# Attention with beacons, then soft experts: other first loads and beacon loads, a reordered start, row sums among the output

## The chip, the cores and the metric

One NeuronCore of a Trainium2 chip runs one program. It has five engines with instruction streams of their own: TensorE (PE, with its weight loads as PEld), VectorE (DVE), ScalarE (ACT), GpSimd (POOL) and SyncE (SP), and 16 DMA engines that move data between HBM and SBUF on behalf of queues: SP's, ACT's and POOL's. PE reads SBUF and writes PSUM; DVE and ACT read and write both; POOL works on SBUF. The metric is the device time of one execution in microseconds; lower is better. TensorE's clock is granted in steps and shown by the profile (1.00 is full).

## The reference

Eight batches of eight heads, 576 tokens, 64 channels, with 16 beacon keys and values ahead of the causal ones:

```python
k_all = concatenate([beacon_k, k], axis=2)          # (8, 8, 592, 64)
v_all = concatenate([beacon_v, v], axis=2)
scores = q @ k_all.T / 8                            # causal mask on the 576, none on the beacons
a = exp(scores - max); a /= a.sum + 1e-9
x = (a @ v_all)  -> (4608, 512)                     # heads side by side

logits = x @ phi                                    # (4608, 32): 8 experts of 4 slots
d = softmax of logits over the 4608 tokens;  c = softmax over the 32 slots
slot_out[e] = relu((d.T @ x)[e] @ w1[e]) @ w2[e]    # w1 (512, 1024), w2 (1024, 512), per expert
out = c @ slot_out                                  # (4608, 512)
```

All inputs and the output are float32: q, k and v 9.4 MB each, the experts' weights 33.6 MB, the output 9.4 MB.

## The kernel before

The kernel keeps q, k and the scores' exponentials in half precision and takes no maximum; a flag computed at the end chooses a general path if the sums ever leave their range. The work on x is laid out by pairs of heads: 32 pairs (`n`), four to a batch (`b, g = divmod(n, 4)`). The order of all five instruction streams is written out by hand (`tc.manual_schedule`, L666): what is emitted first on an engine runs first there, and SP and POOL issue their DMAs in the same way, in order.

**Loads.** `load_qk(b, hb)` (L344) brings k and q of four heads, two heads a row of partitions, as 2304 byte pieces on 128 partitions. `load_v(b)` (L355) brings v so that partition p holds four successive rows of every head, shifted by the 16 beacon rows; partitions 0 to 3 are the beacons' place. For batch 0 it asks for partitions 4 to 116 and 116 to 128, for the others for all 128, whose first four are then overwritten by `load_bv(b)` (L380), 32 KB on 4 partitions. As that overwrites, SP waits for v before it issues it. `load_vr` (L376) brings the last 80 rows in 256 byte pieces. The beacon keys of all batches come once, on 64 partitions (L669). The expert weights are cast from float32 on the way, 32 requests of 512 KB (in float16) on POOL's queue (`load_weights`, L442), one or two after each pair; the last 12 go into buffers that q, k and v no longer need (`wt`, `wv`).

**Start (L699 to L744).** PE first runs `fill` matmuls without use of their result, turns k and q of the first half batch (`transposes`, L466: PE into PSUM tiles of the tag "tr", of which there are two, then DVE and ACT back to SBUF), turns the beacon keys through PSUM into `bkA` (L712), from which POOL copies the 16 columns of each pair ahead of k (`beacon_keys`, L459). Then come scores and exponentials of pairs 0 and 1, four banks each (`scores`, L508: PE, then ACT's exp from a "sc" tile, of which there are two; `select`, L497: POOL masks). v is cast by POOL (`cast_v`, L384, pieces 0, 1 and the remainder 2) and its rows are put in token order by `perm_v` (L396): 16 matmuls with quarter-array 0/1 matrices `sel` into four banks, then ACT and DVE copy to `vh`.

**Loop (L746).** For n = 2 to 31: scores of pair n, transposes of a later half batch, the weighted sums of pair n-1 (`attend`, L525), their division (`normalize`, DVE), turning x (`x_transposes`), once a batch the logits (L572), the slots' inputs (`dispatch`, L604) and the turned weights `eT` (`combine_T`, L636); casts and `perm_v` of the next batch at g = 1 to 3 (for batch 1 at g = 2 and 3, that is at pairs 2 and 3); loads of batch b+2 at g = 0 and 2.

**End.** After the last pair PE does the first expert products (`first`), turns them, does the second ones (`second`, L827) into `so`, which DVE divides into `so1` (L863). `row_sums(bb)` (L659) computes the softmax denominators of a quarter of the tokens, nine matmuls of one column; `row_factors` (L840) turns two quarters at a time into reciprocals. The output stage (L901) is 36 matmuls, each scaled by ACT or DVE into `osb` (six buffers) and stored by SP in 13 requests. POOL's range tests (L880) run beside it, and `judge` (L891) combines them.

## Time and profile before

| | |
|---|---|
| Time, median of 3 runs | 203.09 us (202.74 to 204.77) |
| The profiled execution | 203.09 us, of which the span 201.4 us |
| Busy: PE, DVE, ACT, POOL | 163.2, 132.2, 133.9, 113.9 us |
| Granted TensorE clock, mean | 0.95 |
| HBM read, written | 62.69 MB, 9.44 MB |
| DMA, mean over the span | 278 GB/s |
| First exponential of pair 0, of pair 2 | 12.20, 23.81 us |
| Start of the output's matmuls | 171.86 us |

Times inside the execution count from the start of the span. GB/s are bytes written by the DMA engines: a weight load that casts reads twice what it counts. A line such as "POOL L390 CAST vc<-vstag 128x512 f16<-128x512 f32 x4" names the engine, the line of the kernel, the operation, what is written from what, the shapes, and how many instructions were merged; in brackets stands the idle time before and what ended it.

### The profile page before, as it was taken

The page shows a single profiled execution, that of the slowest core. Times are in us where ns is not written, and L with a number is a line of the kernel's source. Part 1 is how long each engine was busy: PE and PEld are TensorE (multiplying, and loading weights), DVE is VectorE, ACT ScalarE, POOL GpSimd, SP SyncE. Part 2 cuts the span into 40 slices and gives each one's busy share as a digit, 9 for nine tenths or more (in the row PEclk, how much of TensorE's full clock was granted, in tenths as well). Part 3 has the DMA queues.
Part 4 walks back from the last instruction along what each step waited for, and adds up shares of the span by engine and source line. Part 5 has one row for each costly group of instructions (what it writes and reads, how often), then busy time and mean ns, then how long its engine had stood idle before and what let it go on. Part 6 is the DMA issues. An engine that isn't in the chain of part 4 may idle for free.

```text
span 201.4 us, 7361 instructions
## 1 busy us (share of the span) xinstructions
PE 163.2 (81%) x3121; PEld 107.9 (54%) x3121; DVE 132.2 (66%) x275; ACT 133.9 (66%) x172; POOL 113.9 (57%) x263
## 2 busy tenths in 40 slices
PE   6798893889889898988988899898989997966200
PEld 2433661668567476666756667675767753522000
DVE  0352784688987888887887878878837332898300
ACT  2355784689878888889887788987895230774200
POOL 6049186469649757865965786898786000890000
PEclk9999999799999999999999999999999999995855
DMA  6999999999999999999999999999999991499991
GB/s 206 254 244 365 278 361 317 270 370 311 267 271 378 264 261 349 292 275 305 356 232 279 379 273 268 264 219 217 211 216 212 213 202 30 176 410 417 408 405 78
DMA packets 29701, 55.90 MB, mean 278 GB/s; under 512 B 7228, under 2 KB 15644, under 8 KB 29660
## 3 DMA queue, kind: packets, MB, share of 16 engines
q1 hardware_dynamic: 24764, 37.98, 55.4%
q0 software_dynamic: 4608, 16.78, 41.7%
q10 hardware_dynamic: 288, 0.59, 1.0%
q8 instruction: 26, 0.43, 0.8%
q14 instruction: 15, 0.12, 0.2%
HBM read 62.69 MB, written 9.44 MB: 358 GB/s over the span
## 4 chain that ended last, share of the span: by engine, by line
PE 60%; DMA 10%; ACT 9%; DVE 8%; POOL 3%; issue 3%; SPq 0%; ACTq 0%; DVEq 0%; POOLq 0%
PE sc L514 15%; PE av L535 15%; PE trps L483 9%; DMA wt<-in_moe_w_dram 7%; ACT expT L519 5%; PE xtps L561 5%; DVE osb L918 4%; ACT vh L407 4%; PE vpt L404 2%; DMA kstag<-in_k_dram 2%; PE fill L655 2%; PE fps L911 2%; PE lgps L580 2%; PE vps L404 2%; PE sips L619 2%
## 5 line engine op out<-in xcount | busy, mean ns | idle before, releaser
L519 ACT ACTIVATE expT<-sc 128x992 f16<-128x992 f32 (+3 forms) x128 | 104.8, 867 | 20.6 <-PE sc L514 20.0
L505 POOL TENSOR_SCALAR_AFFINE_SELECT expT<-expT 128x224 f16<-128x224 f16 (+3 forms) x128 | 54.9, 439 | 40.1 <-ACT expT L519 39.2
L514 PE MATMUL sc<-qT,kT 64*128 64x80 bf16 (+4 forms) x576 | 43.8, 246 | 10.8 <-ACT expT L519 5.5
L535 PE MATMUL av<-vh,expT 128*128 128x65 f16 (+1 forms) x960 | 40.4, 195 | 0.4 <-DVE x L549 0.2
L535 PEld LDWEIGHTS <-expT 128*128 128x128 f16 (+1 forms) x960 | 33.7, 98 | 4.5 <-POOL expT L505 0.6
L495 DVE COPY kT<-trps 128x640 bf16<-128x640 bf16 (+1 forms) x31 | 22.7, 773 | 19.8 <-PE trps L483 19.3
L514 PEld LDWEIGHTS <-kT 64*128 64x128 bf16 x576 | 17.0, 95 | 28.1 <-issue 22.2
L495 DVE COPY qT<-trps 128x640 bf16<-128x640 bf16 (+1 forms) x30 | 22.0, 774 | 8.2 <-PE trps L483 6.3
L549 DVE TENSOR_TENSOR x<-av,r 128x640 f16<-128x640 f32 x32 | 26.4, 825 | 1.1
L390 POOL CAST vc<-vstag 128x512 f16<-128x512 f32 x32 | 18.6, 611 | 1.8 <-DMA vstag<-in_beacon_v_dram 1.8
L916 ACT ACTIVATE osb<-fps,rc 128x512 f32<-128x512 f32 (+1 forms) x18 | 11.0, 678 | 12.2 <-PE fps L911 10.9
L568 DVE COPY xT<-xtps 128x576 f16<-128x576 f16 x31 | 14.2, 457 | 6.5 <-PE xtps L561 6.5
L561 PE MATMUL xtps<-idh,x 128*128 128x128 f16 (+2 forms) x160 | 14.1, 216 | 1.1 <-issue 1.0
L918 DVE TENSOR_SCALAR osb<-fps,rc 128x512 f32<-128x512 f32 (+1 forms) x19 | 12.8, 731 | 1.3 <-PE fps L911 1.1
L655 PE MATMUL fill<-eT,onesh 128*128 128x512 f16 x35 | 11.4, 453 | 1.7 <-POOL onesh L684 1.5
L407 ACT ACTIVATE vh<-vps 128x1024 f16<-128x1024 f32 x8 | 8.2, 1027 | 6.6 <-PE vpt L404 6.6
L561 PEld LDWEIGHTS <-x 128*128 128x128 f16 (+2 forms) x160 | 9.0, 97 | 6.6 <-issue 6.0
L410 DVE CAST vh<-vpt 128x512 f16<-128x512 f32 x16 | 10.3, 685 | 3.4 <-PE vpt L404 3.4
L911 PE MATMUL fps<-so,eT 128*128 128x512 f16 (+1 forms) x37 | 11.6, 433 | 0.5 <-DVE stat L841 0.3
L462 POOL COPY kT<-bkA 64x32 bf16<-64x32 bf16 x32 | 7.4, 231 | 7.9 <-DVE bkA L712 6.9
L483 PE MATMUL trps<-idb,kstag 128*64 128x128 bf16 x270 | 11.6, 234 | 0.1
L483 PE MATMUL trps<-idb,qstag 128*64 128x128 bf16 x270 | 10.7, 222 | 0.5 <-DVE vh L410 0.4
(98 smaller groups left out, 186.7 us busy)
## 6 DMA issues: line engine op xcount, KB each, us to landing
kstag<-in_k_dram SPq DMA_DIRECT2D x15, 576.0 KB, 9.4
qstag<-in_q_dram SPq DMA_DIRECT2D x15, 576.0 KB, 13.4
out_dram<-osb SPq DMA_DIRECT2D x11, 768.0 KB, 7.6
vstag<-in_v_dram SPq DMA_DIRECT2D x7, 1024.0 KB, 15.3
w1h<-in_moe_w_dram POOLq DMA_DIRECT2D x10, 512.0 KB, 8.6
w2h<-in_moe_w_dram POOLq DMA_DIRECT2D x10, 512.0 KB, 8.5
wt<-in_moe_w_dram POOLq DMA_DIRECT2D x8, 512.0 KB, 12.2
wv<-in_moe_w_dram POOLq DMA_DIRECT2D x4, 512.0 KB, 11.6
```

Of the source, the lines that this page charges most:

```text
L390: nc.gpsimd.tensor_copy(out=st["c", b][:, :, hs, :].rearrange("p t h d -> p h t d"), in_=st["v", b][:, hs, :, :])
L407: nc.scalar.activation(vhs[b % 2][:, 0:2, :, 0:D], ps[:, :, :].rearrange("p c (h d) -> p c h d", d=D), AF.Copy)
L483: nc.tensor.transpose(tp[lo:hi, j - j0, :], t[:, hh, j, :].bitcast(BF)[:, 1::2], idb[:, :])
L495: nc.vector.tensor_copy(out=do, in_=ti)
L505: nc.gpsimd.affine_select(out=ap, in_=ap, compare_op=AL.is_ge, fill=0.0, base=cbase, pattern=pat, channel_multiplier=-1)
L514: nc.tensor.matmul(sc[:, hh, col:col + qw], kTs[n // 2 % 2][po:po + D, n % 2, c * P:(c + 1) * P], qTs[n // 2][po:po + D, n % 2, q0:q0 + qw ...
L519: nc.scalar.activation(ex[:, :, base:base + w], sc[:, :, 0:w], AF.Exp, scale=scale)
L535: nc.tensor.matmul(av[:, i, :], exps[n % 2][0:KW[c], hh, o:o + P], vhs[b % 2][0:KW[c], c, h, :], start=(c == 0), stop=(c == i))
L549: nc.vector.tensor_tensor(out=xs[b][:, :, head(n, 0):head(n, 1) + 1:head(n, 1) - head(n, 0), :].rearrange("p i h d -> p h i d"), in0=av[:, ...
L561: nc.tensor.transpose(tp[:, QLO[i]:QLO[i] + QW[i]], xs[b][0:QW[i], i, 2 * t:2 * t + 2, :].rearrange("p h d -> p (h d)"), idh[0:QW[i], 0:QW ...
L911: nc.tensor.matmul(f[:, 0:hw], row_tokens(bb, j), so1[:, hw * i:hw * i + hw], start=True, stop=True)
L918: nc.vector.tensor_scalar(out=ou, in0=f[:, 0:hw], scalar1=rc[:, bb, j:j + 1], scalar2=None, op0=AL.mult)
```

## The change

- `load_v(0)` asks for heads 1 to 7 on all 128 partitions in one request, and for head 0 in two (partitions 4 to 64, 64 to 128); POOL clears head 0's first four partitions. No beacon value is written into v's tile any more: `load_bv` is gone.
- The beacon values come twice on their own: those of batch 0 on 16 partitions (`bv0`), those of all batches on 128 (`bvf`, 256 byte pieces). POOL casts each into `bvh`, the second at pair 3. `sel` loses the rows of the first four partitions, and `perm_v` gets one more matmul, which adds the beacon rows from `bvh`.
- The beacon keys come on 128 partitions, half as long; DVE alone casts them, ahead of q's copy; 16 transposes instead of 32. The first pair's 16 columns are copied by DVE straight from PSUM, `bkA` is filled afterwards.
- SP's order: k and q of batch 1's first half ahead of its v.
- At the start: q's first transposes go into the "av" banks, as does batch 0's `perm_v`; the second piece of batch 0's v is cast by DVE; `perm_v(0)` comes right behind the first scores of pair 1; fewer fills; `sel` is built ahead of the first fill.
- The exponential of the logits is written once by ACT and copied three times by DVE in every batch, not only in the last.
- `row_sums` has its own PSUM tile and computes its reciprocals at once. Quarters 2 and 3 move from around `second(1)` into the output stage, behind the third request of quarters 0 and 1. POOL's test of the sums moves behind the other two tests, into `judge`.
- The last weight piece is asked for in two requests. One fill more ahead of the last `x_transposes`.

```diff
     def load_v(b):
...
-        if b:
...
-        else:
-            for p0, p1 in ((4, 116), (116, 128)):
+        h0 = 0 if b else 1
+        lo = ((b * H + h0) * S - Nb) * D
+        nc.sync.dma_start(
+            out=t[:, h0:H, :, :].rearrange("p h t d -> p h (t d)"),
+            in_=v.rearrange("b h s d -> (b h s d)")[lo:lo + (H - h0) * S * D].rearrange(
+                "(h e) -> h e", h=H - h0)[:, 0:4 * P * D].rearrange("h (p e) -> p h e", p=P))
+        if b == 0:
+            nc.gpsimd.memset(t[0:4, 0, :, :], 0.0)
+            for p0, p1 in ((4, 64), (64, 128)):
                 nc.sync.dma_start(
...
-    def load_bv(b):
...
-                nc.gpsimd.tensor_copy(
+                (nc.vector if c == 1 and b == 0 else nc.gpsimd).tensor_copy(
...
     def perm_v(b):
-        ps = ps_sc.tile([P, 2, 512], FP, name="vps", tag="sc")
+        pool, tag = (ps_sc, "sc") if b else (ps_av, "av")
+        ps = pool.tile([P, 2, 512], FP, name="vps", tag=tag)
...
+            if t == 0:
+                lhsT, rhs = (idh[:, b::B], bvh) if b else (idh[0:Nb, 0:Nb], bvh[0:Nb])
+                nc.tensor.matmul(outs[0][0:Nb, :], lhsT, rhs[:, :, :].rearrange("p h d -> p (h d)"),
+                                 start=False, stop=False)
...
+                cs = 2 if (e, m, j) == WLAST else 4
+                for c in range(0, 4, cs):
+                    nc.gpsimd.dma_start(
...
-        if t0 == 0:
-            nc.scalar.activation(dTs[b][:, :, :, :],
-                                 lp[:, :, :].unsqueeze(2).broadcast_to([P, NC5, 4, NSL]), AF.Exp)
-        else:
...
+        nc.scalar.activation(dTs[b][:, :, 0, :], lp[:, :, :], AF.Exp)
+        nc.vector.tensor_copy(
+            out=dTs[b][:, :, 1:4, :],
+            in_=dTs[b][:, :, 0:1, :].broadcast_to([P, NC5, 3, NSL]))
...
+    def row_sums(bb, rsp):
         for j in range(NJ):
...
+        sl = slice(bb * NJ, bb * NJ + NJ)
+        nc.vector.tensor_scalar(out=rsv[:, sl], in0=rsp[:, 0:NJ], scalar1=1e-9, scalar2=None,
+                                op0=AL.add)
+        nc.vector.reciprocal(out=rcf[:, sl], in_=rsv[:, sl])
...
         load_v(0)
-        load_bv(0)
+        bv0 = work.tile([P, H, D], FP, name="bv0", tag="x")
+        nc.sync.dma_start(out=bv0[0:Nb, :, :], in_=beacon_v[0].rearrange("h n d -> n h d"))
         load_vr(0)
         load_qk(0, 1)
+        load_qk(1, 0)
         load_v(1)
-        load_qk(1, 0)
-        load_bv(1)
         load_vr(1)
+        bvf = work.tile([P, H, D], FP, name="bvf", tag="x")
+        nc.sync.dma_start(out=bvf[:, :, :], in_=beacon_v.rearrange("b h n d -> n b h d"))
...
         fill(10, False)
         transposes(0, 0)
-        fill(2, False)
+        bkh = work.tile([P, Nb // 2, D], BF, name="bkh", tag="vc", bufs=1)
+        nc.vector.tensor_copy(out=bkh[:, :, :], in_=bkf[:, :, :].bitcast(BF)[:, :, 1::2])
         transposes(0, 1)
...
+        beacon_keys(0, bkp[:, :, :].rearrange("p n (c a) -> p n c a", a=2), nc.vector)
+        nc.vector.tensor_copy(out=bkA[:, :, :, :].rearrange("p n c a -> p n (c a)"),
+                              in_=bkp[:, :, :])
+        fill(3)
...
-        for c in range(2):
-            cast_v(0, c)
+        cast_v(0, 0)
+        nc.gpsimd.tensor_copy(out=bvh[0:Nb, :, :], in_=bv0[0:Nb, :, :])
+        cast_v(0, 1)
...
         cast_v(0, 2)
-        for bank in range(3):
-            fill(3, False)
-            scores(1, bank)
+        scores(1, 0)
+        perm_v(0)
+        scores(1, 1)
         transposes(1, 0)
-        perm_v(0)
+        scores(1, 2)
+        attend(0, 0)
+        transposes(1, 1)
         scores(1, 3)
-        transposes(1, 1)
-        attend(0, 0)
         attend(0, 1)
...
+            if n == 3:
+                nc.gpsimd.tensor_copy(out=bvh[:, :, :], in_=bvf[:, :, :])
...
-        fill(1)
+        fill(2)
...
-        row_sums(2)
         second(1)
...
-        row_sums(3)
-        row_factors(2 * NJ, 4 * NJ)
...
+        test(so1, Dm, -SUM_HI)
+        test(sz1, NDC * NSL, -SUM_HI)
         def judge():
+            test(stat, NST + 36 + 1, SUM_LO)
...
                 nc.sync.dma_start(out=outr[bb, :, j0:j1, :], in_=osb[:, 0:j1 - j0, :])
+                if bb in (0, 1) and j0 == 3:
+                    row_sums(bb + 2, ps_g.tile([P, NJ], FP, name="rsps", tag="g"))
```

More of the change, by code (lines that the diff above doesn't have):

```diff
@@ L308 @@
     phih = const.tile([P, NDC, NSL], F16, name="phih")
-    bkA = const.tile([P, Nb, B * H], BF, name="bkA")
+    bkA = const.tile([P, Nb // 2, B * H, 2], BF, name="bkA")
+    bvh = const.tile([P, H, D], F16, name="bvh")
     NRES = 5
@@ L476, in transposes @@
             dst = kTs[m % 2][:, :, Nb:Nb + S]
+        if (m, which) == (0, 1):
+            two = ps_av.tile([P, 2, 512], FP, name="trps", tag="av")
         for j0, j1 in ((0, 5), (5, NJ)):
-            tp = ps_tr.tile([P, j1 - j0, P], BF, name="trps", tag="tr")
+            if (m, which) == (0, 1):
+                tp = two[:, j0 // 5, :].bitcast(BF)[:, 0:(j1 - j0) * P].rearrange(
+                    "p (j s) -> p j s", s=P)
+            else:
+                tp = ps_tr.tile([P, j1 - j0, P], BF, name="trps", tag="tr")
             for j in range(j0, j1):
@@ L686 @@
         make_identity(nc, idh)
+        nc.gpsimd.memset(sel[:, :, :], 0.0)
         for t in kTs:
@@ L695 @@
         nc.gpsimd.memset(xT[:, :, S:640], 0.0)
-        nc.gpsimd.memset(sel[:, :, :], 0.0)
-        fill(10, False)
-        transposes(0, 0)
-        fill(2, False)
-        transposes(0, 1)
-        bkh = work.tile([P, Nb, D], BF, name="bkh", tag="vc", bufs=1)
-        hi = bkf[0:B * H, :, :].bitcast(BF)[:, :, 1::2]
-        nc.scalar.activation(bkh[0:B * H, 8:Nb, :], hi[:, 8:Nb, :], AF.Copy)
-        nc.vector.tensor_copy(out=bkh[0:B * H, 0:8, :], in_=hi[:, 0:8, :])
-        bkp = ps_tr.tile([P, Nb, B * H], BF, name="bkps", tag="tr")
-        for i in range(Nb):
-            for hh in range(2):
-                nc.tensor.transpose(bkp[64 * hh:64 * hh + 64, i, :], bkh[0:B * H, i, :],
-                                    idb[0:B * H, 0:B * H])
-        nc.vector.tensor_copy(out=bkA[:, :, :], in_=bkp[:, :, :])
-        beacon_keys(0)
-        fill(5, False)
         for c in range(4):
@@ L800 @@
         logits(B - 1, NDC - 1, NDC)
-        row_sums(0)
+        row_sums(0, ps_tr.tile([P, NJ], FP, name="rsps", tag="tr"))
         sp = dispatch(B - 1, sizv)
@@ L835, in second @@
                         stop=(eg == E // 4 - 1 and c == NFC - 1))
[L837 to L845 removed]
+        row_sums(1, ps_av.tile([P, 2, 512], FP, name="rsps", tag="av")[:, 0, :])
         first(0, 0)
[L847 removed]
         first(0, 1)
@@ L879, with test @@
         tests = []
-        for src, w, low in ((stat, NST + 36 + 1, SUM_LO), (so1, Dm, -SUM_HI),
-                            (sz1, NDC * NSL, -SUM_HI)):
+        def test(src, w, low):
             lo = gd.tile([P, w], FP, name="lo", tag=f"lo{w}")
```

73 lines of the change are left out of this document (31 added, 42 removed).

## The prediction

> **What bounds the kernel now.** I read the end first, in the chain that ended last (start, length, what).
>
> ```profile
> 154.15 14.88 DMA wt<-in_moe_w_dram
> ...
> 169.08 1.04 PE rsps L831 x13
> 170.15 0.76 DVE so L863
> ...
> 170.95 0.66 PE rsps L663 x9
> ...
> 171.63 0.19 DVE stat L841
> ...
> 171.86 0.61 PE fps L911 x3
> ```
>
> The last piece of expert weights lands at 169.0; PE finishes the second expert product, DVE scales it into `so1`, PE does the last row sums, DVE reads them, and only at 171.86 can the output start. The table by stages (stretch; its length, busy time of PE, PEld, DVE, ACT, POOL; clock; DMA share; GB/s) and the waits say whether transfers or engines are late:
>
> ```profile
> 6.00:14.00 8.00, 6.75 (x91) 3.64 (x91) 4.50 (x20) 3.75 (x6) 1.00 (x3) 1.00 1.14 216
> 14.00:22.00 8.00, 6.86 (x83) 2.86 (x83) 2.85 (x5) 5.52 (x8) 5.66 (x14) 1.00 1.05 366
> 22.00:26.00 4.00, 3.77 (x94) 2.94 (x94) 3.19 (x6) 2.99 (x5) 1.00 (x3) 1.00 0.96 267
> ...
> 34.00:38.00 4.00, 3.24 (x45) 2.30 (x45) 2.46 (x4) 2.52 (x4) 1.18 (x4) 0.57 1.07 225
> ...
> 38.00:152.00 114.00, 103.39 (x2349) 74.98 (x2347) 91.51 (x184) 97.28 (x122) 82.35 (x191) 1.00 1.07 284
> 152.00:166.00 14.00, 13.63 (x268) 9.23 (x268) 7.05 (x21) 4.67 (x8) 3.26 (x6) 1.00 1.04 210
> ...
> 174.00:198.00 24.00, 9.60 (x29) 3.75 (x27) 13.00 (x23) 9.26 (x15) 6.80 (x8) 0.72 0.99 397
> ```
> ```profile
> PE rsps L831 <- DMA wt<-in_moe_w_dram: 0.6, 1, 0.6
> ...
> PE sc L514 <- ACT vh L407: 4.6, 7, 0.8
> ...
> PE vps L404 <- POOL vc L390: 2.4, 1, 2.4
> ...
> SPq L381 <- DMA vstag<-in_v_dram: 39.2, 7, 6.6
> ```
>
> Two things run neck and neck to 169 us. The transfer engines are full from 6 to 166 us (share about 1), so all loads end when their total work is done. PE is busy 103.4 of 114 us in the loop and waits for the last weights only 0.6 us. A gain therefore needs **both**: fewer transfer microseconds and an earlier loop. From 174 to 198 us the stores are the limit (397 GB/s); what moves the first store moves the end.
>
> **The start.** Next the timeline (start, length, engine, line, operation, idle before).
>
> ```profile
> 7.06 0.83 DVE L495 COPY kT<-trps 128x640 bf16<-128x640 bf16 x1 [7.06 <-PE trps L483]
> ...
> 9.19 0.41 DVE L706 COPY bkh<-bkf 64x512 bf16<-64x512 bf16 x1
> ...
> 10.41 0.69 DVE L712 COPY bkA<-bkps 128x1024 bf16<-128x1024 bf16 x1 [0.81 <-PE bkps L710]
> ...
> 11.17 0.56 POOL L462 COPY kT<-bkA 64x32 bf16<-64x32 bf16 x2 [6.94 <-DVE bkA L712]
> ...
> 12.20 3.14 ACT L519 ACTIVATE expT<-sc 128x992 f16<-128x992 f32 x4 [2.32 <-PE sc L514]
> ...
> 13.50 2.28 POOL L390 CAST vc<-vstag 128x512 f16<-128x512 f32 x4 [1.77 <-DMA vstag<-in_beacon_v_dram]
> ...
> 15.71 2.90 ACT L519 ACTIVATE expT<-sc 128x992 f16<-128x992 f32 x3 [0.37 <-PE sc L514]
> ...
> 20.57 1.03 ACT L407 ACTIVATE vh<-vps 128x1024 f16<-128x1024 f32 x1 [1.97 <-PE vpt L404]
> ...
> 21.49 0.70 ACT L519 ACTIVATE expT<-sc 128x640 f16<-128x640 f32 x1
> ...
> 22.40 0.74 ACT L493 ACTIVATE qT<-trps 128x512 bf16<-128x512 bf16 x1 [0.21 <-PE trps L483]
> ...
> 23.81 5.21 ACT L519 ACTIVATE expT<-sc 128x992 f16<-128x992 f32 x6 [0.67 <-PE sc L514]
> ```
>
> First scores. Now the beacon keys go qT, bkh, bkA, POOL one after another. Afterwards DVE does `bkh` ahead of qT: 7.89 + 0.41 + 0.83 (qT's first half has kT's form) = 9.13, while PE turns the beacon keys; two small DVE copies straight from PSUM replace bkA and POOL on the path. Their form is not shown; 0.19 us (DVE's small read of PSUM, stat in the first fence) and 0.28 each (the POOL row) bound them, I take 0.2. Scores at about 9.8, the first exp at 10.5 instead of 12.2: 1.7 us. `bkA` moves behind and is used only in the loop; the 16 `sel` copies move into DVE's 7.06 idle us.
>
> First v. The first cast starts at 13.5, when v has landed. With v on all 128 partitions the transfers ahead are some 2.4 us shorter (worked out below): 11.2, a little of it left to the landing. POOL casts two pieces (1.2 us), then `bvh` (0.6, the form of the same row), DVE the other two at once: ready at 13.0. ACT runs from 10.5 the four exps of pair 0 (3.14) and the first of pair 1 (1.0 of the 2.90 for three) to 14.65, the turned v (1.03) to 15.9, exps of banks 1 and 2 (1.7, as PE follows at once) to 17.6; qT waits for DVE's v and kT copies to free PSUM: 18.05 to 18.8; exp of bank 3 (0.7) to 19.5. So the loop's first exp stands at 19.5 instead of 23.8: 4.3 us. I laid no handover between engines into this, and take **3.7**; 2.2 if v comes no earlier, 4.3 at most.
>
> The Trainium skill, SBUF — State Buffer, section "SBUF: two separate sides", says that a GpSimd operation and a DVE one in a two-port mode hold a shared port for a whole instruction, so the two halves of the cast would not run together. By it v would be ready near 14.3, the 3.7 would be 3.0 and the time 200.7, within the range of the forecast; the trace of before has no such pair.
>
> **The loop.** A row of the timeline and then rows of the chain around the second v:
>
> ```profile
> 31.39 1.17 POOL L390 CAST vc<-vstag 128x512 f16<-128x512 f32 x2
> ```
> ```profile
> 32.61 0.39 PE vps L404 x2
> ...
> 33.01 0.21 PE vps L404 x2
> ...
> 33.70 1.02 ACT vh L407
> ```
>
> And the table of stages by batches:
>
> ```profile
> 33.70:51.66 17.96, 15.96 (x325) 11.23 (x322) 13.92 (x28) 14.47 (x19) 10.88 (x27) 0.90 1.07 304
> ...
> 68.93:85.80 16.87, 15.61 (x353) 11.42 (x353) 14.27 (x29) 14.47 (x19) 11.80 (x29) 1.00 1.07 295
> ```
>
> The change adds one matmul of 512 columns to every `perm_v`. PE, then ACT's vh copy, then PE's next scores are the chain there (0.8 us of wait in each batch), so nothing hides it. A step of four quarter-array matmuls costs 0.21, the first step 0.39; one matmul over the whole array costs at least the 0.21, and breaks the packing of the quarters, at most the first step again: I take 0.28, so 7 x 0.28 = **2.0** lost (1.5 to 2.7).
>
> At pair 3 POOL casts `bvh` before the second half of v (0.6 us); select, `bvh`, cast, `perm_v` stand in a row and PE already waits 2.4: **0.6** lost. Queued behind the copy on POOL are those casts, the next selects and the weight requests. It needs the all-batch beacon load, which I expect near 24 us, some 3 us before. No wait is hidden there if it is late.
>
> The logits' exp shrinks fourfold on ACT, and a copy comes to DVE that the last batch has already (first row; the second is DVE's next work behind the logits of batch 0):
>
> ```profile
> 157.88 0.31 DVE L590 COPY dT<-dT 128x480 f16<-128x480 f16 x1 [0.78 <-ACT dT L589]
> ...
> 48.14 1.45 DVE L495 COPY qT<-trps 128x640 bf16<-128x640 bf16 x2 [0.61 <-PE trps L483]
> ```
>
> Its 0.31 us fit into the 0.61 that DVE waits there, and ACT is not what the chain waits for: nothing. Without this cover it would be 0.31 a batch. POOL's beacon key copies keep their size.
>
> **Transfers.** From 6 to 14 us 1.73 MB (8 x 216) moved at 216 GB/s; at the 366 of the next stretch this takes 4.7 us, so up to 3.3 us can be won. In this stretch go v on 112 and 12 partitions, its beacon on 4, the remainder on 80. The request on 112 becomes one on 128, as the later v (14 to 22 us) has it; the remainder stays: I take 2.4 of 3.3. SP waits 39.2 us for v before the small beacon loads; without them it issues on, and the dip at 22 to 26 us, (366-267) x 4 / 366 = 1.1 us, goes for half: 0.6. The beacon load for all batches moves 262 KB in 256 byte pieces; between 366 and 216 GB/s that is 0.7 to 1.2 us, against 0.6 for the seven it replaces: at the slow end -0.6. Sum **2.4** (1.0 to 3.5). k and q of batch 1 ahead of the second v cost nothing: v's first cast comes at the end of pair 2, and the bytes ahead of it end before 22 us.
>
> **The sum at `so1`.** PE: 3.7 - 0.6 - 2.0, plus 0.65 for the row sums taken out ahead of `second(1)`, minus 0.2 for one more fill (a step of 512 columns) = 1.55; and PE no longer waits its 0.57: 2.1. Transfers: 2.4, and with the last piece in two requests PE has only two of four steps left after the landing, 2 x 0.21 = 0.4: 2.8. The later counts: **2.1**. POOL pays one more request, after which it only clears a tile.
>
> **The output.** It no longer waits for the last row sums: from 170.95 to 171.86 is **0.95** with the handover. Their two replacements fall among the stores, 0.65 us of PE and some 0.45 of DVE each (stat 0.19 and the reciprocal in the first row here):
>
> ```profile
> 171.84 0.27 DVE L843 RECIPROCAL rc<-stat 128x18 f32<-128x18 f32 x1
> ...
> 171.90 1.13 POOL L884 TENSOR_SCALAR lo<-stat 128x357 f32<-128x357 f32 x1 [12.62 <-DVE stat L841]
> ...
> 180.49 1.27 ACT L916 ACTIVATE osb<-fps,rc 128x512 f32<-128x512 f32 x2 [1.24 <-DMA out_dram<-osb]
> ...
> 158.64 0.29 DVE L622 SCALAR_TENSOR_TENSOR siz<-sips,acc 128x128 f16<-128x128 f32 x1 [0.46 <-PE sips L619]
> ```
>
> Here ACT already waits for free buffers, so stores hide them; without that cover they would cost 1.1 us each. The factors of the first row sums fit DVE's 0.46 idle us before siz. POOL's test of the sums (three passes of at most the 1.13 of the POOL row, 3.4 us) moves behind the other two and still ends near 181, when DVE judged before; late, it would hold up DVE, with the stores' buffers as cover.
>
> Together 2.1 + 0.95 = 3.05. The profiled execution took 203.09, its span 201.4 and 1.7 around it; it is also the median of the runs. **203.09 - 3.05 = 200.0.**
>
> **The rivals.**
> 1. *The loop takes it back.* The inserted matmul costs more (0.4, total 2.8) and the longer wait at pair 3 costs another window of half clock. For it: after the wait of 2.4 us the clock was 0.57 from 34 to 38, and the batch took 17.96 instead of 16.87, 1.1 us. Against: one such window is paid already. 3.05 - 0.8 - 1.1 = 1.15: 201.9. The Trainium skill, TensorE: Matmul & The Clock Gate, section "Why this matters for your kernels", asks for idle gaps under about 3 us; the trace halves the clock after 2.4 us already, so by the trace the present window counts, by the rule a first one would.
> 2. *The first v is no faster*, the change not doing what it says: start 2.2 and transfers 0.9, so 0.6 + 0.95: 201.5. For it: the 256 byte remainder shares the slow stretch.
> 3. *Better.* A matmul at 0.21 and no half clock: PE 3.7, transfers at 2.8 to 3.5 decide: 198.6 to 199.3.
> 4. *Slower.* POOL stands in order behind the all-batch beacon load. It is behind about 6.5 MB (k and q of three half batches, two v with remainders, the beacon keys, its own); from 2.5 us on it lands near 24 at 330 GB/s, near 33 at 216. Pair 3 needs it about 27.5 (31.39 less the 3.7); every microsecond beyond delays selects, casts and PE; from 30.5 the gain is gone, at 33 the loss is 5.5 - 3.05 = 2.5: 205.5. Against: only one stretch was that slow.
>
> **Chances.** Forecast 0.5 (199.2 to 201.0), first rival 0.18, second 0.1, third 0.15, fourth 0.07. Under 201.06 lie the forecast, the third and a few hundredths: faster by over 1% (about what a measurement of this kernel can tell from no change) 0.68; within 1% 0.25; slower 0.07. The range 198.5 to 202.7 leaves out the fourth and the ends of the first and third, under 0.2.
>
> **What would show it.** First exp at 10.5; loop's first exp near 20; over 320 GB/s from 6 to 14 us; `perm_v` about 0.3 longer; PE's wait for vc at 3.0; PE and the last weights still within 1 us of each other near 167; fps within 0.1 of so1; stores without gaps near 400 GB/s. A gap in the stores, a POOL wait for the beacons, or a second half-clock window would make the number wrong.

## The result, and the profile after

The changed kernel took 204.19 us in the median of 20 executions (200.72 to 205.48); the kernel before, beside it, 204.45 (202.69 to 206.63). The ratio is 0.990, with a 95% interval of 0.986 to 0.994, where the forecast was 200.0 / 203.09 = 0.985. The executions of the changed kernel lie in two groups, nine from 200.7 to 203.5 and eleven from 204.2 to 205.5, of which the ratio counts the first alone, while both traces of it (204.46 with a span of 202.7, and 204.02) are of the second; what sets the two apart stays open. By the medians over all executions the change is worth 0.1%, by the ratio 1%, about what a measurement can tell from no change. The median lies outside the forecast's range of 198.5 to 202.7.

The table by stages of the kernel after (length; busy time of PE, PEld, DVE, ACT, POOL; clock; DMA share; GB/s):

```profile
6.00:14.00 8.00, 6.50 (x86) 3.65 (x85) 4.85 (x9) 4.29 (x6) 3.18 (x6) 1.00 1.10 340
14.00:22.00 8.00, 7.17 (x147) 4.58 (x148) 5.87 (x10) 7.12 (x9) 4.00 (x11) 1.00 1.09 301
22.00:26.00 4.00, 3.53 (x85) 2.58 (x82) 3.09 (x7) 3.73 (x5) 3.86 (x9) 1.00 1.02 342
26.00:30.00 4.00, 1.06 (x21) 0.53 (x17) 1.47 (x4) 1.02 (x2) 3.81 (x9) 0.78 1.10 355
30.00:34.00 4.00, 3.42 (x30) 1.03 (x29) 1.29 (x2) 2.00 (x3) 0.42 (x2) 0.50 1.06 288
34.00:38.00 4.00, 4.00 (x64) 3.21 (x60) 2.29 (x5) 1.56 (x2) 2.00 (x5) 0.50 1.07 258
38.00:152.00 114.00, 103.60 (x2290) 72.84 (x2289) 92.41 (x187) 92.68 (x118) 82.59 (x186) 1.00 1.06 276
152.00:166.00 14.00, 13.36 (x245) 8.98 (x245) 6.43 (x22) 5.59 (x10) 5.51 (x11) 0.88 1.06 213
...
174.00:198.00 24.00, 10.70 (x52) 5.35 (x49) 14.25 (x28) 10.53 (x17) 7.90 (x9) 0.81 0.97 390
```

The early transfers did what was hoped: 340 GB/s instead of 216 from 6 to 14 us. But the clock column shows half speed from 28 to 38 us, where the kernel before has 0.57 for four microseconds, and a second dent between 152 and 166. The start and pair 3 in the timeline of the kernel after:

```profile
10.59 1.17 POOL L386 CAST vc<-vstag 128x512 f16<-128x512 f32 x2 [6.09 <-DVE kT L467]
...
11.00 2.56 ACT L532 ACTIVATE expT<-sc 128x992 f16<-128x992 f32 x3 [0.81 <-PE sc L527]
11.17 1.62 DVE L386 CAST vc<-vstag 128x512 f16<-128x512 f32 x2
11.71 0.80 POOL L741 CAST bvh<-bv 16x512 f16<-16x512 f32 x1
...
19.34 2.49 ACT L532 ACTIVATE expT<-sc 128x640 f16<-128x640 f32 x3
...
27.62 0.61 POOL L784 CAST bvh<-bvf 128x512 f16<-128x512 f32 x1
28.18 1.18 POOL L386 CAST vc<-vstag 128x512 f16<-128x512 f32 x2
...
29.41 0.61 PE L401 MATMUL vps<-vc,sel 32*128 32x512 f16 x2 [2.94 <-POOL vc L386]
```

The first exp stands at 11.0 (before 12.2). The row at 19.34 is the last exp of pair 1 and the first two of pair 2, so pair 2 begins at 19.99, its instruction taken alone, instead of 23.81. At pair 3 PE waits 2.94 us, as forecast. Then the timeline of one undisturbed `perm_v`, first before (L404 the quarter steps), then after (L401 the quarter steps, L406 the inserted matmul):

```profile
50.41 0.39 PE L404 MATMUL vps<-vc,sel 32*128 32x512 f16 x2
50.42 0.73 PE L404 MATMUL vpt<-vc,sel 32*128 32x512 f16 x2
50.79 0.39 PE L404 MATMUL vps<-vc,sel 32*128 32x512 f16 x2
...
51.65 1.03 ACT L407 ACTIVATE vh<-vps 128x1024 f16<-128x1024 f32 x1 [0.36 <-PE vpt L404]
```
```profile
102.57 0.39 PE L401 MATMUL vps<-vc,sel 32*128 32x512 f16 x2
102.58 0.73 PE L401 MATMUL vpt<-vc,sel 32*128 32x512 f16 x2
103.24 0.40 PE L406 MATMUL vps<-bvh,idh 128*16 128x512 f16 x1
103.58 0.39 PE L401 MATMUL vps<-vc,sel 32*128 32x512 f16 x2
...
103.80 0.38 PE L401 MATMUL vps<-vc,sel 32*128 32x512 f16 x2
...
104.44 1.03 ACT L408 ACTIVATE vh<-vps 128x1024 f16<-128x1024 f32 x1 [0.99 <-PE vpt L401]
```

From the first matmul to ACT's copy it takes 1.87 us instead of 1.24: 0.63 a batch. The starts show where. In both kernels the last quarter of the first step starts 0.36 us behind the other three (the row of 0.73 us holds two matmuls of some 0.38). Before, the second step starts beside that late quarter, 0.37 behind the first step. After, the inserted matmul stands between: it starts 0.30 behind the late quarter, and the second step 0.34 behind it, 1.00 behind the first. The steps after that follow every 0.22 in both kernels. So 0.34 is the matmul, and 0.30 the late quarter, which no longer runs beside a step. Last the end, in the chain of the kernel after:

```profile
161.24 3.36 PE hps L833 x32
...
169.41 2.73 PE so L848 x48
172.17 0.76 DVE so L870
172.98 1.46 PE fps L919 x7
174.43 0.48 PE rsps L672 x9
```

No weight stands in this chain any more: `so1` comes at 172.17 behind PE's own work, 2.0 us later than before instead of 2.1 earlier. The output follows it by 0.05 us, as the change meant. The 32 matmuls at 161.24 (the first expert product) take 3.36 us; they took 1.9 before, and a half-clock window of 3.4 us begins at 161.4.

The copies of the turned v mark the batches. Timeline of the kernel after, then of the one before:

```profile
32.00 1.03 ACT L408 ACTIVATE vh<-vps 128x1024 f16<-128x1024 f32 x1 [4.72 <-PE vpt L401]
51.26 1.03 ACT L408 ACTIVATE vh<-vps 128x1024 f16<-128x1024 f32 x1 [0.99 <-PE vpt L401]
...
140.02 1.03 ACT L408 ACTIVATE vh<-vps 128x1024 f16<-128x1024 f32 x1 [0.99 <-PE vpt L401]
```
```profile
33.69 1.03 ACT L407 ACTIVATE vh<-vps 128x1024 f16<-128x1024 f32 x1 [2.64 <-PE vpt L404]
51.65 1.03 ACT L407 ACTIVATE vh<-vps 128x1024 f16<-128x1024 f32 x1 [0.36 <-PE vpt L404]
...
137.34 1.03 ACT L407 ACTIVATE vh<-vps 128x1024 f16<-128x1024 f32 x1 [0.36 <-PE vpt L404]
```

With `so1` at 170.15 and 172.17 the time up to it divides into four parts (us, after less before; the forecast by the prediction's own terms):

| Part | before | after | difference | forecast |
|---|---|---|---|---|
| to `vh` at pair 3 | 33.69 | 32.00 | -1.7 | -3.7 + 0.6 + 0.28 = -2.8 |
| next batch | 17.96 | 19.26 | +1.3 | +0.3 |
| five batches | 85.69 | 88.76 | +3.1 | 5 x 0.28 = +1.4 |
| to `so1` | 32.81 | 32.15 | -0.7 | -0.65 - 0.57 + 0.2 = -1.0 |
| sum | | | +2.0 | -2.1 |

Five batches lose 0.61 each. Of the 1.1 us missing in the first row and the 1.0 in the second, 0.33 each are the insertion, which cost 0.61 instead of 0.28; the rest lies where the clock is halved. In the other trace of the change the half clock falls later: `vh` stands at 30.98 and the next batch ends at 51.86, against 51.26 here. The last row hides some 1.1 us of half clock at 161: the kernel with the fills and one fill, which has no window there, takes 31.02 for it.

### The profile page after: what moved, and what is told of

Its sections match the earlier page's. It is cut to its first block, busy times and chain, and to the rows that moved or that the text cites. A ratio compares the mean times of both kernels' runs of the same rounds, so it can differ in the third digit from the quotient of the medians.

```text
span 202.7 us, 7336 instructions
## 1 busy us (share of the span) xinstructions
PE 164.7 (81%) x3101; PEld 107.9 (53%) x3101; DVE 137.7 (68%) x291; ACT 131.5 (65%) x171; POOL 117.9 (58%) x263
## 4 chain that ended last, share of the span: by engine, by line
PE 68%; ACT 12%; DVE 6%; POOL 4%; issue 3%; ACTq 0%; DVEq 0%; POOLq 0%
PE sc L527 14%; PE av L548 14%; PE trps L496 8%; ACT expT L532 6%; PE xtps L574 5%; PE vps L401 5%; ACT vh L408 4%; PE fill L664 3%; PE fps L919 3%; PE hps L833 3%; PE sips L628 2%; PE lgps L593 2%; PE so L848 2%; DVE osb L926 2%; POOL expT L518 2%
## 5 line engine op out<-in xcount | busy, mean ns | idle before, releaser
L548 PE MATMUL av<-vh,expT 128*128 128x65 f16 (+1 forms) x960 | 41.2, 195 | 0.5 <-issue 0.5
L548 PEld LDWEIGHTS <-expT 128*128 128x128 f16 (+1 forms) x960 | 34.2, 99 | 4.4 <-issue 1.7
L386 POOL CAST vc<-vstag 128x512 f16<-128x512 f32 x30 | 17.5, 613 | 6.1 <-DVE kT L467 6.1
L926 DVE TENSOR_SCALAR osb<-fps,rc 128x512 f32<-128x512 f32 (+1 forms) x19 | 12.8, 725 | 1.0 <-PE fps L919 0.8
L401 PE MATMUL vps<-vc,sel 32*128 32x512 f16 x64 | 10.5, 408 | 2.9 <-POOL vc L386 2.9
L401 PE MATMUL vpt<-vc,sel 32*128 32x512 f16 x64 | 12.6, 408 | 0.0
L919 PE MATMUL fps<-so,eT 128*128 128x512 f16 (+1 forms) x37 | 10.9, 421 | 1.2 <-DVE so L870 0.9
## 6 DMA issues: line engine op xcount, KB each, us to landing
qstag<-in_q_dram SPq DMA_DIRECT2D x15, 576.0 KB, 12.2
wt<-in_moe_w_dram POOLq DMA_DIRECT2D x7, 512.0 KB, 10.2
```

The costliest lines, as they stand in the source:

```text
L386: (nc.vector if c == 1 and b == 0 else nc.gpsimd).tensor_copy(out=st["c", b][:, :, hs, :].rearrange("p t h d -> p h t d"), in_=st["v", b][ ...
L401: nc.tensor.matmul(outs[c], sel[32 * c:32 * c + 32, t, :], vc[32 * c:32 * c + 32, t, :, :].rearrange("p h d -> p (h d)"), start=(t == 0), ...
L548: nc.tensor.matmul(av[:, i, :], exps[n % 2][0:KW[c], hh, o:o + P], vhs[b % 2][0:KW[c], c, h, :], start=(c == 0), stop=(c == i))
L919: nc.tensor.matmul(f[:, 0:hw], row_tokens(bb, j), so1[:, hw * i:hw * i + hw], start=True, stop=True)
L926: nc.vector.tensor_scalar(out=ou, in0=f[:, 0:hw], scalar1=rc[:, bb, j:j + 1], scalar2=None, op0=AL.mult)
```

## The experiments

Two theories were tested. Theory A: the inserted matmul costs 0.6 a batch, and the longer wait at pair 3 brings more half clock; together they take the start's gain back. Theory B: the transfers set the end, whatever PE does. In each experiment one execution was traced; "median" is over all executions of its kernel there.

**The change once more.** 

> The changed kernel as it is, beside the others on the same chip. Both theories: between 0.98 and 1.00 of the kernel before. Theory A (the loop takes the start's gain back: the inserted matmul costs 0.6 us a batch, and the wait at pair 3 costs three windows of half clock instead of one): first exp of pair 2 near 20.2 against 23.8, perm_v 1.8 us against 1.2, clock 0.5 in a stretch between 28 and 39 us. Theory B (transfers set the end, whatever the loop does): PE waits for the last weights by 1 us or more.

Median 204.03 of 6 (200.91 to 208.3), ratio 0.986 (0.976 to 0.997), `so1` at 171.70. This is the reference on this chip for the next two.

**Without the insertion.** It leaves out the beacon values of batches 1 to 7.

```diff
-            if t == 0:
+            if t == 0 and b == 0:
```

> The changed kernel without the inserted matmul in batches 1 to 7 (their beacon values are left out of the sums). Theory A: perm_v back to 1.2 us, seven times 0.6 = 4.4 us off the loop; the end follows until the last weights are the later, 2 to 3.5 us below the changed kernel. Theory B: less than 1 us, with PE waiting for the weights all the longer.

Median 201.16 (199.66 to 201.56), 2.9 under the change; `so1` comes at 169.37. The ratio to the kernel before is 0.984 (0.977 to 0.990), which doesn't set it apart from the change's 0.986: the difference is in the medians and in the traces. Undisturbed batches take 16.7 again (68.52 to 85.21 here), so the insertion is worth the 0.6. PE still waits 2.9 us at pair 3, and the half clock is still there.

**PE kept busy at pair 3.**

```diff
                 if g == 3:
+                    if b == 0:
+                        fill(12)
                     perm_v(b + 1)
```

> The changed kernel with 12 fill matmuls on PE ahead of the perm_v of pair 3, where PE waits 2.9 us for POOL's casts; nothing else. Theory A: clock 1.00 through from 8 to 180 us, batches of 17 us from the first on, 2 to 3.5 us below the changed kernel. Rival to its clock part (the halved windows have another cause, for example the turned k and q): the clock falls all the same and the time stays within 0.7 us.

Median 201.40 (200.16 to 201.85), 2.6 under the change, ratio 0.985 (0.979 to 0.991; again not apart from 0.986). All six lie under 202, where four of the change's six beside it were above 204. The stages of this kernel, and of the one after with the same cut:

```profile
26.00:40.00 14.00, 11.80 (x201) 7.04 (x195) 8.66 (x19) 9.09 (x12) 8.42 (x19) 1.00 1.07 301
```
```profile
26.00:40.00 14.00, 10.03 (x137) 5.71 (x134) 6.21 (x13) 6.55 (x9) 6.87 (x16) 0.63 1.07 306
```

The turned v still waits for POOL's cast, so the fills win nothing there; but the clock stays at 1.00, and `so1` comes at 169.31 instead of 171.70 and 172.17: the half clock behind the wait is worth 2.4 to 2.9 us in these traces. The window at 158 us is still there.

**The same in the kernel before** (10 fills).

> The kernel before with 10 fill matmuls at the same place (its wait there is 2.4 us and one window of half clock follows). Theory A: the window at 34.5 us goes; the batch from 33.7 us takes 16.9 instead of 18.0; but the last weights set the end there, so only 0.5 to 1 us less in time. If the clock falls for another reason: nothing.

Median 205.11 of 12 against 205.22, ratio 1.002 (0.998 to 1.007): nothing, though in its trace the window is gone, the batch takes 16.7 instead of 17.96 and `so1` stands at 168.87. The first store then leaves 1.3 us earlier, but from there to the end it takes 1.0 us longer in this trace. Why the executions don't gain was not found.

**A second trace of the kernel before.** 

> The kernel before, unchanged, for a second trace of it: the one shown took 203.09 with mean clock 0.950, the median of its later executions is 205.2 at about 0.918. A span of 201.4 at 0.950 holds 20 us at half clock; 203.5 at 0.918 holds 33 us, some four windows of 3.4 us more. Theory A (half-clock windows that start at pair 3 set the time): in an execution near 205 the window at 34.5 us is 10 us long instead of 3.4, the batch from the first vh to the second takes 18.9 to 19.3 instead of 17.96, so1 ends near 172 instead of 170.9. Rival: the added windows lie behind 174 us, among the stores, and the time above 203 comes from slower stores (25.5 us or more from the first store to the last packet instead of 24.8); then so1 stays near 170.9 and windows at pair 3 say nothing of before's median.

203.9 us, `so1` at 170.81, clock 0.88 from 26 to 40 us as in the first trace, and one more window near 22 us. It did not fall on one of the executions near 205, so neither side of the expectation was decided.

**Where the insertion stands.** First with the 12 fills, as a quarter of the array in the same place:

```diff
+                g0 = 32 * (b // 2)
-                lhsT, rhs = ((idh[:, b::B], bvh) if b
+                lhsT, rhs = ((idh[g0:g0 + 32, Nb * b:Nb * b + Nb], bvh[g0:g0 + 32]) if b
```

> After with 12 fills ahead of perm_v at pair 3, and the beacon rows inserted by a matmul of one quarter of the array (32 rows in, 16 columns) instead of all 128 rows; bvf is laid out batch by batch for it with eight small loads. Theory A (the full-array matmul costs its own 0.33 us and makes the next quarter step start over, 0.63 a batch): a quarter matmul joins the packed steps, 0.2 or less a batch, undisturbed batches 16.9 instead of 17.33, so1 near 166.5 to 167.5, time 201.4 - 7 x 0.4 = 198.6 where nothing else sets the end. Rival (any matmul put between the steps costs 0.6, because they write one bank): batches stay at 17.3 and the time at 201.4. Theory B (transfers set the end): last weights at 167.6 as in the kernel with the fills alone, so1 no earlier than 168.5, time not under 200.6.

Its undisturbed batch is 17.30 us (87.78 to 105.08): no cheaper, so the rival's time was right. Its reason, the one bank, isn't shown by this: the small matmul also differs in form from the steps (16 columns instead of 128), and no run tried one of the steps' own form in this place. The starts are as in the change: the inserted matmul 0.30 behind the late quarter, the second step 0.31 behind the matmul. Ahead of the steps, starting the bank's sum:

```diff
+        lhsT, rhs = (selb[:, :], bvh) if b else (idh[0:Nb, :], bvh[0:Nb])
+        nc.tensor.matmul(outs[0], lhsT, rhs[:, :, :].rearrange("p h d -> p (h d)"),
+                         start=True, stop=False)
         for t in range(4):
             for c in range(4):
...
-                                 start=(t == 0), stop=(t == 3))
+                                 start=(t == 0 and c > 0), stop=(t == 3))
```

> After with 12 fills ahead of perm_v at pair 3, and the beacon rows inserted by a full-array matmul of all 128 columns that stands ahead of the quarter steps and starts the sum of the first bank; a small tile with the selecting columns is written by DVE before each batch. Theory A in its two halves (own 0.33 us; second entry into the quarter steps 0.3): only the first remains, undisturbed batches 17.0 instead of 17.33, so1 near 167.2, time 199.3. If the whole 0.63 is the matmul itself wherever it stands: 17.3 and 201.4. Theory B: not under 200.6.

The timeline of this kernel:

```profile
99.38 0.39 PE L401 MATMUL vps<-bvh,selb 128*128 128x512 f16 x1
99.70 0.39 PE L405 MATMUL vps<-vc,sel 32*128 32x512 f16 x2
99.70 0.41 PE L405 MATMUL vpt<-vc,sel 32*128 32x512 f16 x2
99.92 0.38 PE L405 MATMUL vps<-vc,sel 32*128 32x512 f16 x2
...
100.78 1.03 ACT L408 ACTIVATE vh<-vps 128x1024 f16<-128x1024 f32 x1 [0.53 <-PE vpt L405]
```

From 99.38 to 100.78 are 1.40 us, 0.16 over the kernel before instead of 0.63, and undisturbed batches take 16.87. Behind this matmul all four quarters of the first step start together, and the second step follows 0.22 later, so the late quarter costs nothing here and gives back half of the matmul's 0.32. `so1` came at 167.16 and the traced execution took 198.93, the shortest of all runs; the six lie at 198.9, 200.5 and four times 209.9 to 211.1. The quarter form had the same: 205.3, 206.1 and four times 211 to 214. The experiment on all three repairs comes back to that.

Without the fills:

> After with the beacon rows inserted by a full-array matmul of 128 columns ahead of the quarter steps, without fills at pair 3. With fills this form took 198.9 to 200.5 us in some executions and 210 to 211 in others; its traced batch was 16.87 instead of 17.33. Theory A: seven batches at 0.45 less are 3.2 us under after, 200.9. Rival on the slow executions: if they come from the inserted matmul's form (and not from the fills or from that chip), some of these runs also take 10 us more, 211 to 214; if none does, the fills with it are needed for that.

Median 201.56 (199.39 to 202.94), ratio 0.986 (0.979 to 0.992), and none near 210. In its trace the half clock is as long as without the insertion (0.59 from 26 to 40 us), undisturbed batches take 16.86, and PE waits 0.6 us for the last weights again: the transfers are reached.

**The cast at pair 3 on ACT.**

```diff
             if n == 3:
-                nc.gpsimd.tensor_copy(out=bvh[:, :, :], in_=bvf[:, :, :])
+                nc.scalar.activation(bvh[:, :, :], bvf[:, :, :], AF.Copy)
```

> After with the cast of bvh at pair 3 on ACT, which waits for perm_v at that place, instead of on POOL ahead of the second half of v. PE's wait for vc there should be 2.3 to 2.4 us instead of 2.94. Theory A (three windows of half clock follow a wait of 2.9 us, one follows a wait of 2.4, as in the traces of before): one window of 3.4 us near 31 us, so1 0.6 + 1.8 us earlier (170.0 instead of 171.7 to 172.2), time 201.6 to 202. Rival (the number of windows has nothing to do with the wait's length): still about 10 us at half clock, time 203.4 to 204.

PE's wait is 2.4 us, the clock 0.76 from 26 to 40 us (two windows of 3.4), the median 202.0 of 12 (200.27 to 204.31), ratio 0.988 (0.984 to 0.992). With 2.4 us of wait the four traces show one or two windows (0.88, 0.88, 0.76, 0.76 in that stretch), with 2.6 to 2.9 us three or four (0.69, 0.63, 0.59, 0.58). So longer waits went with more windows in these eight traces, though not as one window for each 0.6 us, and not without end: two traces further down have a wait of 8.1 and 8.2 us, and 10.2 us of half clock behind it, three windows.

**The window at 158 us.**

```diff
         dispatch(B - 2)
-        fill(2)
+        fill(1)
```

> After with 12 fills ahead of perm_v at pair 3, and one fill instead of two behind dispatch(6), as the kernel before has it. In every trace with the change a half-clock window of 3.4 us falls on the first expert product (158 to 164 us), which then takes 3.5 instead of 1.9 us, though PE does not wait before it; in the traces of before none falls there. Theory C (the second fill brings it on): no window there, so1 1.6 us earlier, time 201.4 - 1.6 = 199.8. Rival (it comes from long unbroken work, wherever the kernel stands at 158 us): the window stays, time 201.2 to 201.4.

With the fills at pair 3 and this, median 200.84 (199.98 to 202.35), ratio 0.987 (0.980 to 0.993); the trace has no window at 158, the first product takes its short time and `so1` comes at 167.92. But both kernels with the insertion ahead and two fills there have no window, and the next one, which has one fill, has a window (0.72 from 158 to 164 us). So the second fill does not decide it; what does stays open.

**The output part alone, in the kernel before.**

```diff
         second(0, NFC // 2)
-        row_sums(2)
         second(1)
...
-        row_sums(3)
-        row_factors(2 * NJ, 4 * NJ)
...
                 nc.sync.dma_start(out=outr[bb, :, j0:j1, :], in_=osb[:, 0:j1 - j0, :])
+                if bb in (0, 1) and j0 == 3:
+                    late_sums(bb + 2)
```

`late_sums` is the change's `row_sums`, and the test of the sums moves behind the other two as there.

> The kernel before with the last part of the change alone: the row sums of the last two blocks of output stand among the output, the test of the sums behind the other two. Where the first store waits for so1 it goes out 2.7 us after so1's start, as in the traces of after, instead of 3.9: 1.2 us earlier, plus at most 0.65 us of row sums taken out ahead of the second expert product, of which the last weights (169 us) give back all but 0.4. If the stores set the end from there at the same length (24.8 us): 1.2 to 1.6 us under before, ratio 0.993. Rival (the added PE and DVE work between the stores holds them up): stores take 25.5 us or more and the time is that of before within 0.5.

Median 202.11 of 11 against 204.56, ratio 0.992 (0.988 to 0.996). Its chain, and the first store's request in its timeline, then in those of the kernels before and after:

```profile
170.08 0.76 DVE so L862
170.88 1.46 PE fps L921 x7
172.34 0.48 PE rsps L893 x9
```
```profile
171.92 10.95 SPq L932 DMA_DIRECT2D out_dram<-osb  x10
```
```profile
173.17 9.41 SPq L922 DMA_DIRECT2D out_dram<-osb  x9
```
```profile
174.01 8.38 SPq L930 DMA_DIRECT2D out_dram<-osb  x8
```

From `so1` to that request are 1.84 us here and 1.84 in the change, 3.02 before: 1.2 won. From the request to the end of the span are 28.28 us here, 28.69 after and 28.23 before: the row sums among the stores cost 0.1 to 0.5. In all sixteen traces this last stretch takes 28.2 to 29.2 us, so what moves `so1` moves the time. Alone this part gives a ratio of 0.992, as expected; the whole change gives 0.990, so most of what it gains may be this part.

**All three repairs.** Insertion ahead, fills at pair 3, one fill at the end.

> After with all three repairs: insertion ahead of the quarter steps, 12 fills ahead of perm_v at pair 3, one fill instead of two behind dispatch(6). Theory A: so1 near 167, time 198.9 to 199.5 where the executions are the undisturbed ones; PE is then within 1 us of the last weights (166.2), so that no more than 1 us is left to win before the transfers decide. Rival (the slow executions of this form return): median near 210.

Median 209.44 (202.5 to 211.12). This time one of the long executions was traced, and in it PE waits for transfers, as in theory B. First its transfers from 126 to 142 us (queue: packets, MB, share of the engines' time), then PE's longest wait (total, times, longest):

```profile
DMA packets 1578, 3.81 MB, mean 238 GB/s; under 512 B 517, under 2 KB 517, under 8 KB 1576
...
q0 software_dynamic: 765, 2.81, 87.1%
q1 hardware_dynamic: 811, 0.96, 19.3%
```
```profile
PE trps L500 <- DMA kstag<-in_k_dram: 8.2, 1, 8.2
```

POOL's queue (q0) brings weights, SP's (q1) the last k, q and v. Over this stretch both move about as many packets, but a weight packet writes 3.7 KB and one of k, q and v 1.2 KB in the mean, and the weights take 87% of the engines' time. The last k, asked for at 118.6 us, comes at 146; PE has been waiting since 138.2. In the execution of 198.93 the k was asked for at 109.8 and came at 128.0. The late request alone is not enough: the kernel before asks for its last k at 118.1 and has no such wait. SP's requests in the long execution fall behind those of the short one from about 34 us on (2.8 us there, 9 at the end), and its transfers are slower, 286 to 290 GB/s from 47.5 to 99.4 us instead of 299 to 306; which of the two brings the other, and why, isn't known. The Trainium skill, DMA: Bandwidth & Descriptors, section "Queues, rings and completion order", says that each engine takes turns between its queues by the packet. The counts of 765 and 811 are near that, but within the stretch they are not equal (146 and 393 from 126 to 130 us, 325 and 159 from 136 to 142), so this trace doesn't settle it. To test it, two weight requests of batch 6 were put off:

```diff
-            load_weights((0, 1, 1, 1)[g] if b < 6 else 2)
+            load_weights((0, 1, 1, 1)[g] if b < 6 else (1, 1, 2, 2)[g] if b == 6 else 2)
```

> The kernel with the three repairs, and in batch 6 one weight request in each of the first two pairs instead of two (six in the batch instead of eight, the other two later). In the trace of the three repairs at 210 us, PE waits 8.2 us at 138 us for the last k, which was asked for at 118.6; from 126 to 142 the weights' queue has 87% of the engines' time with 765 packets and the other queue 19% with 811. Theory B (the loop has caught up with the transfers; two queues share the engines packet by packet, so that late k and v stand behind weights): the wait shrinks to 0 to 5 us, since half a megabyte to one megabyte of weights (2 to 4 us) stands behind k instead of beside it; executions near 200 to 206 instead of 209 to 211. Rival (the 10 us come from the chip, whatever the order of the requests): executions near 210 as without it.

The six executions take 201.12 to 205.91, median 203.5. The end of the traced one (202.04) has the price of it, PE's wait for the weights put off:

```profile
PE so L853 <- DMA wt<-in_moe_w_dram: 1.5, 2, 0.9
```

And beside it the same kernel without the delay:

> The kernel with the three repairs once more, beside the one that holds weights back: 202.5 to 211 by theory B, with PE's wait for the last k of some 8 us in every execution above 208; if the slow executions belong to the chip of the earlier runs, 199 to 200 here.

These take 200.3, 204.9 and four times 208.4 to 210.8, with this wait, 8.1 us long, in the traced one (209.6).

Only the order of the weights differs, and the executions above 206 are gone. So the weights' place decides whether the long wait comes. How it does so is argued: the traced execution with the weights put off asked for its last k at 110.9 and is not of the late kind. A reading that fits is that a loop with `so1` 3 us earlier than before meets the transfers, and whether k arrives ahead of the weights then hangs on a few microseconds. For the quarter form this isn't shown: its eight small loads leave 136 GB/s from 22 to 26 us, so there the transfers may be late rather than PE early; its long executions weren't traced.

The best kernel with no such executions is the change with the fills and one fill at the end: 200.84, under the kernels before and after.

## Why the prediction was wrong

**What bounds.** PE and transfers neck and neck was right, and the kernel after is on PE's side of it: its last weights land at 169.34, and PE, whose last product runs from 169.41 to 172.14, doesn't wait for them. The transfers show as the other bound only where the loop is repaired (PE waits 0.3 us for the last weights in the execution of 198.93, 0.6 without its fills).

**The start** held. Pair 2's first exp came 3.8 us earlier; 3.7 was taken. With the half clock away (fills and one fill) `vh` at pair 3 stands at 30.81, 2.9 earlier; the forecast was 2.8. The first exp at 11.0 was 0.5 later than worked out, the first v 0.6 earlier (cast from 10.59, ready at 12.8). DVE's first cast in the kernel after, and in the one with the insertion ahead and fills, where it starts less than 0.1 us before POOL's cast ends:

```profile
11.17 0.88 DVE L386 CAST vc<-vstag 128x512 f16<-128x512 f32 x1
```
```profile
11.54 0.42 DVE L387 CAST vc<-vstag 128x512 f16<-128x512 f32 x1
```

Beside a POOL cast the same cast takes twice as long, and POOL's `bvh` takes 0.80 instead of the 0.61 at pair 3. Their ends follow each other: POOL at 11.77, DVE at 12.04, POOL at 12.51, DVE at 12.79. So the two take turns, as the rule on the shared port of the Trainium skill (SBUF — State Buffer, "SBUF: two separate sides") has it. By that rule the prediction had v ready at 14.3; it was ready at 12.8, as DVE needs only some 0.3 for a cast between two of POOL's.

**The inserted matmul: the first failed step.** "I take 0.28, so 7 x 0.28 = 2.0" measured 0.61 to 0.63 a batch, 4.3 in all, outside the 1.5 to 2.7 that the prediction allowed. The matmul itself (0.34) lies within its bounds of 0.21 and 0.39. What it left out is the 0.30 for the late quarter. The row that it read, at pair 3, doesn't show that quarter: there and in one more batch of the kernel before the four quarters start together, in the other five of the loop the last is 0.36 late. 2.3 of the 4.1 us by which the sum at `so1` was missed are this.

**The half clock: the second.** The term 0.6 for the wait at pair 3 was right (2.94 us). Its consequence was put into the first rival with one more window, 1.1 us. Instead 10 us at half clock followed, with the insertion itself inside, and 2.4 to 2.9 us were lost against the same kernel without them; one window of 3.4 us stands in before's trace already. The window on the first expert product, 1.1 to 1.4 us, was not in the sum at all, and what brings it is open. The Trainium skill's TensorE: Matmul & The Clock Gate, section "Why this matters for your kernels", warns of gaps of more than about 3 us; here 2.4 us cost one or two windows and 2.9 us three or four, so the measurement is the stricter.

**The first rival** had the mechanism, dearer matmul and more half clock, and gave it 0.18. Both were priced too low: it still left 1.15 us of gain (201.9). By the traced spans the change lost 1.3 us, by the medians it gained 0.3.

**Transfers: the third.** From 6 to 14 us (340 - 216) x 8 = 0.99 MB more were moved; from 14 to 22 us 0.52 less, from 22 to 26 us 0.30 more and to 38 us some 0.1 less, in all 0.6 to 0.7 MB, which at 284 GB/s is 2.3 us: the head start of 2.4 was right. It didn't last to the end, as "all loads end when their total work is done" had it. From 38 to 152 us the kernel after moves 276 GB/s instead of 284, 0.9 MB less. The weights' requests stand in POOL's order of work and come with the loop:

```profile
156.15 1.08 POOL L457 DMA_DIRECT2D wt<-in_moe_w_dram  x2 [0.15 <-issue]
```

Before, the last request went out at 154.15 and landed at 169.04; after, the second of these two goes out at 156.70 and lands at 169.34. With the fills and one fill, where the loop is faster, it goes out at 153.91 and lands at 167.24. It did not decide the time of the change, because PE was later still.

**The output** gave 1.2 (0.95 was taken), less 0.1 to 0.5 among the stores. The stores ran at 390 GB/s instead of 397.

**The base.** 203.09 was a short execution of the kernel before; over 20 the median is 204.45. A forecast on that base would have been 201.4, still 2.8 under what was measured.

**The signs** named for a wrong number were the right ones: more half clock is in the stage table, `perm_v` is 0.63 and not 0.3 longer, PE and the last weights are not near 167. POOL didn't wait for the beacons, and the fourth rival's late load didn't occur.

## What to carry to other kernels

A matmul put between steps that run as packed quarters costs itself and what it keeps from running side by side: here 0.63 us in the two forms tried, and 0.16 ahead of the row. Before pricing such a step, look at the starts of several of its occurrences, not at one. Price a PE wait of more than 2 us by the half clock that follows it in the trace, not by its length, and try dummy work on PE there if the wait can't go; measure it, as in the kernel before the same fills brought `so1` forward by 1.3 us and the time by nothing. A transfer that is won at the start is kept only if the later requests don't wait for the loop. When a loop nears its transfers, look at which late load will stand beside a full queue before making the loop faster.

## What the runs showed that was not expected

- A quarter-array matmul of 16 columns between quarter steps costs as much as a full-array one: 17.30 and 17.33 us a batch, 16.87 with the insertion ahead, 16.7 without any.
- Half clock behind a PE wait comes in pieces of 3.4 us. There were one to four of them after 2.4 to 2.9 us, and three after 8.2 us.
- From 126 to 142 us one queue with 765 packets of 3.7 KB had 87% of the engines' time and another with 811 of 1.2 KB 19% (the two overlap a little). A load of 576 KB took from 118.6 to 146 us.
- Casts of 128x512 from float32 to half precision on DVE and POOL at the same time took turns: 0.88 us instead of 0.42 on DVE.
